# Reordering the first loads of a gated attention and token-MLP kernel: w1 tile 1 ahead of x tile 2, and the bias row off ScalarE's queue

## The chip, the cores and the metric

The kernel runs on one core of one Trainium2 chip. The metric is the device time of one execution in microseconds; before the change it is 163.06 us, the median of three runs that lie between 162.8 and 163.33. One further execution was recorded by the hardware profiler, and all times inside the kernel come from it. Its clock zero is the first instruction of the program.

## What is computed

An input x of 2048 rows and 512 columns (bf16) goes through two branches, and a gate per row mixes them.

```python
g = sigmoid((x * gate_w).sum(-1, keepdims=True))
a = linear_attention(x, wqkv, wo)          # 32 heads of 16
h = layernorm(x)                           # per row, over the 512 columns
u = gelu(einsum("bsd,sf->bdf", h, w1) + b1)   # w1: 2048 x 1792
y = einsum("bdf,fs->bds", u, w2) + b2
out = g * a + (1 - g) * transpose(y)
```

Only the start matters here: the layernorm of x, and the product of w1 with it, which contracts over the 2048 rows.

## The kernel before, in words

x, its layernorm and w1 are cut into 16 tiles of 128 rows. `xr[:, t, :]` is x tile t as loaded (128 KB), `xh[:, t, :]` the same tile after the layernorm. Of w1, the first 1024 columns are `w1A` (256 KB for each tile t), used by the first stage; the other 768 columns come later as `w1B`.

**TensorE** first does 18 matmuls on a constant (`warm_ps`). Then the first real stage fills eight accumulators `accA[j]`, j = 0 to 7, one for each 128 columns of w1A. For tiles t = 0 to 11 the loops run over t outside and j inside, so that eight matmuls in a row belong to one tile; the last four tiles are done per accumulator. A matmul (t, j) needs `w1A[:, t, 128 j : 128 j + 128]` as weights and `xh[:, t, :]` as data. All matmuls of the kernel are recorded by one helper and have line L74. The K projection, `kacc`, follows this stage.

**Loads.** All loads are recorded by one helper, line L124, and an engine issues its loads in program order. Nearly all are on SyncE's queue (SP). Ahead of the change SP issues x tile 0, x tile 1, the columns 128 to 1023 of w1A tile 0 (224 KB), then for t = 1 to 15 in turn x tile t+1 and w1A tile t (of tile 1 again only the columns 128 to 1023). b2's row follows w1A tile 4. Then come the gate's weights, the K weights and sixteen transposing loads of x (`xT`). ScalarE's queue (ACT) issues three loads at the start: b1's row, and the first 128 columns of w1A tiles 0 and 1 (32 KB each). Behind them ScalarE runs a square root on a constant (L137), which loads its table.

Each load signals on one of eight semaphores that are handed out in rotation over both queues, in the order of the loads in the built program; a ninth load is issued only after the one that had its semaphore before has landed.

**Layernorm, on VectorE and ScalarE, in an order written out by hand.** For a tile: statistics (`bn_stats`, L197), their sum (`bn_aggr`, L200), the standard deviation on ScalarE (L202), a reciprocal (L208) and the scaling that writes xh (L210). The statistics of the next tile are put between: for t = 1, 2, 3 they are cut in two halves of 256 columns, of which the first stands ahead of the scaling of the tile before.

```python
for t in range(1, NT):
    if t < HALVES:                      # HALVES = 4
        ln_bn(t, 0, D // 2, 0, 2)       # waits for x tile t
        ln_apply(t - 1)                 # reciprocal and scaling: writes xh of tile t-1
        ln_bn(t, D // 2, D, 1, 2)
    else:
        ln_bn(t, 0, D, 0, 1)
        ln_apply(t - 1)
    ln_aggr(t)
```

So on VectorE the first half of the statistics of x tile 2 stands ahead of the scaling of tile 1, and that of x tile 3 ahead of the scaling of tile 2. Behind the sum of tile 8 VectorE turns the two bias rows into columns (L232 to L234); they are first used by the GELU behind accumulator 0.

Of the kernel before, what the change touches and what calls it, by code (L numbers as in the profile page):

```python
# [15 lines left out]
def kernel(  # L16
# [13 lines left out]
    nc = tc.nc  # L30
    P = nc.NUM_PARTITIONS
# [9 lines left out]
    NT = S // P  # L41
    ND = D // P
    NF = F // P
# [4 lines left out]
    FA = NFA * P  # L48
# [5 lines left out]
    w1_view = B_w1.rearrange("(t p) f -> p t f", p=P)  # L54
    w2_view = B_w2.rearrange("(f p) s -> p f s", p=P)
    b1_view = B_b1.rearrange("(f p) -> f p", p=P)
# [9 lines left out]
    def ptile(shape, dt, name):  # L66
        return persist.tile(shape, dt, name=name, tag=name)
# [27 lines left out]
    b_rows = ptile([32, P], BF16, "b_rows")  # L95
# [22 lines left out]
    w1A = wpool.tile([P, NT, FA], BF16, name="w1A", tag="w1st")  # L118
# [4 lines left out]
    def load(o, i, eng=None, **kw):  # L123
        pin((eng or nc.sync).dma_start(out=o, in_=i, **kw))  # L124

    def load_x(t0, t1):
        load(xr[:, t0:t1, :], x_view[:, t0:t1, :])

    def load_w1a(t):
        load(w1A[:, t, :], w1_view[:, t, 0:FA])  # L130


    tbl = work.tile([P, 1], FP32, name="tbl", tag="tbl", bufs=2)
    load(b_rows[0:NF, :], b1_view, nc.scalar)
    load(w1A[:, 0, 0:P], w1_view[:, 0, 0:P], nc.scalar)
    load(w1A[:, 1, 0:P], w1_view[:, 1, 0:P], nc.scalar)
    pin(nc.scalar.activation(out=tbl[:], in_=eps_t[:], func=ACT.Sqrt))  # L137
# [1 line left out]
    load_x(0, 1)  # L139
    load_x(1, 2)  # L140
    load(w1A[:, 0, P:FA], w1_view[:, 0, P:FA])
    for t in range(1, NT):
        if t + 1 < NT:
            load_x(t + 1, t + 2)
        if t == 1:
            load(w1A[:, 1, P:FA], w1_view[:, 1, P:FA])
        else:
            load_w1a(t)
        if t == 4:
            load(b_rows[NF : NF + NT, :], b2_view)  # L150
    load(gw_b[:], gw_row_view.to_broadcast([P, D]))
    load(wk_sb[:], wqkv_view[:, :, D : 2 * D])
# [404 lines left out]
    t = NT - 1  # L557
# [35 lines left out]
```

## Time and profile before

| what | us |
|---|---|
| device time, median of 3 runs | 163.06 |
| span of the profiled execution, first to last instruction | 161.6 |
| difference of the two, for what lies outside the span | 1.5 |
| TensorE busy in the span | 157.1 |
| VectorE busy in the span | 118.7 |
| ScalarE busy in the span | 53.0 |

The profiler gives the span of its own execution; that execution's device time is not given separately, and 1.5 us is the difference of a median and a span. TensorE is busy 97% of the span at a granted clock of 0.998, so the time is the matmuls plus the few places where TensorE stands still. In the views, PE is TensorE, PEld its weight loads, DVE VectorE, ACT ScalarE, POOL GpSimd; SPq and ACTq are queues that issue loads.

### The profile page before, as it was taken

The numbers are of one execution on the slowest core, as the hardware profiler recorded it, in microseconds if no ns is written. First come the engines' busy times: TensorE is split into PE (matmuls) and PEld (weight loads), VectorE is DVE, ScalarE is ACT, GpSimd is POOL, SyncE is SP. The second block draws the span as 40 slices with busy tenths as digits, with TensorE's granted clock in tenths as the row PEclk, the third lists the DMA queues.
The fourth block names the chain that finished last, engine by engine and source line by source line (L and its number), as shares of the span: only waits on it lengthen the run. The fifth ranks groups of instructions, "written<-read, shape, count | busy, mean of one in ns | idle before, by whom it ended". The sixth has DMA issues, their size and how long they took to land.

```text
span 161.6 us, 2275 instructions
## 1 busy us (share of the span) xinstructions
PE 157.1 (97%) x820; PEld 72.9 (45%) x820; DVE 118.7 (73%) x279; ACT 53.0 (33%) x89; POOL 1.2 (1%) x8
## 2 busy tenths in 40 slices
PE   7899999999999999999999999999999999999993
PEld 5344444444444444444444444444444444444452
DVE  2799998959998998799895999999999980000002
ACT  3122226895243221435225970000008300550050
POOL 2000000000000000000000000000000000000000
PEclk9999999999999999999999999999999999999999
DMA  4999998444699540229953007826535925824421
GB/s 140 271 320 353 364 300 144 101 103 106 159 394 390 149 129 0 87 50 310 402 200 67 0 32 230 322 65 143 186 89 136 353 70 143 265 63 105 143 97 32
DMA packets 36966, 28.33 MB, mean 175 GB/s; under 512 B 20572, under 2 KB 31452, under 8 KB 36956
## 3 DMA queue, kind: packets, MB, share of 16 engines
q1 hardware_dynamic: 36368, 27.87, 57.0%
q10 hardware_dynamic: 588, 0.33, 0.7%
q8 instruction: 6, 0.10, 0.3%
q14 instruction: 4, 0.03, 0.1%
HBM read 19.28 MB, written 4.46 MB: 147 GB/s over the span
## 4 chain that ended last, share of the span: by engine, by line
PE 94%; DMA 3%; SPq 1%; DVE 0%; issue 0%; DVEq 0%
PE yps L74 39%; PE accA L74 16%; PE accB L74 13%; PE qacc L74 9%; PE Gps L74 9%; PE kacc L74 9%; DMA w1A<-in_B_w_dram 3%; SPq L124 1%; PE kvps L74 0%; DVE ot L537 0%; PE w2ps L74 0%; DVEq L537 0%
## 5 line engine op out<-in xcount | busy, mean ns | idle before, releaser
L74 PE MATMUL yps<-uT,w2h 128*128 128x512 bf16 (+2 forms) x238 | 49.2, 366 | 0.0
L74 PEld LDWEIGHTS <-w2h 128*128 128x128 bf16 x238 | 22.8, 98 | 25.9
L74 PE MATMUL accA<-xh,w1A 128*128 128x512 bf16 x128 | 28.0, 379 | 0.8 <-DVE xh L210 0.5
L530 ACT ACTIVATE ot<-yps,c,c 128x512 bf16<-128x512 f32 x15 | 11.6, 777 | 46.9 <-PE yps L74 35.5
L74 PE MATMUL accB<-xh,w1B 128*128 128x512 bf16 x96 | 21.5, 379 | 0.0
L537 DVE TENSOR_SCALAR ot<-yps,c,c 128x384 bf16<-128x384 f32 (+1 forms) x2 | 1.1, 545 | 25.5 <-PE yps L74 25.5
L74 PEld LDWEIGHTS <-w1A 128*128 128x128 bf16 x128 | 12.5, 98 | 16.1 <-DMA w1A<-in_B_w_dram 1.4
L74 PEld LDWEIGHTS <-xT 128*128 128x128 bf16 x128 | 12.4, 98 | 14.9 <-issue 0.2
L74 PE MATMUL kacc<-wk_sb,xT 128*128 128x512 bf16 x64 | 15.8, 379 | 0.0
L74 PE MATMUL Gps<-pk,xr 128*128 128x512 bf16 x64 | 15.8, 379 | 0.0
L74 PE MATMUL yps<-W2sb,pqT 128*128 128x512 bf16 (+2 forms) x68 | 14.6, 366 | 0.0
L74 PEld LDWEIGHTS <-w1B 128*128 128x128 bf16 x96 | 9.4, 98 | 11.3
L74 PE MATMUL qacc<-wq_sb,xT 128*128 128x512 bf16 x64 | 14.5, 379 | 0.0
L286 ACT ACTIVATE e<-qacc 128x512 bf16<-128x512 f32 x16 | 9.6, 597 | 12.2 <-DVE kvbdT L434 4.6
L286 ACT ACTIVATE e<-kacc 128x512 bf16<-128x512 f32 x16 | 9.2, 598 | 12.7 <-DVE pk L293 6.8
L197 DVE BATCH_NORM_STATS2 stats<-xr 128x6 f32<-128x512 bf16 (+1 forms) x19 | 11.1, 586 | 2.7 <-DMA xr<-in_A_x_dram 2.7
L288 DVE TENSOR_SCALAR e<-e 128x512 bf16<-128x512 bf16 x32 | 9.2, 288 | 4.6 <-ACT e L286 4.3
L406 DVE SCALAR_TENSOR_TENSOR pq<-pq,odds,rd 128x512 bf16<-128x512 bf16 x16 | 12.0, 752 | 0.6
L402 DVE TENSOR_REDUCE den<-prod 128x32 f32<-128x544 f32 x16 | 11.5, 720 | 0.6
L293 DVE SCALAR_TENSOR_TENSOR pk<-kacc,e 128x512 bf16<-128x512 f32 x16 | 11.1, 692 | 1.0
L293 DVE SCALAR_TENSOR_TENSOR pq<-qacc,e 128x512 bf16<-128x512 f32 x16 | 11.1, 692 | 0.6
L245 DVE CUSTOM_DVE_ANT_0 junk<-xr,gw_b 128x512 bf16<-128x512 bf16 x16 | 11.0, 689 | 0.4
(52 smaller groups left out, 95.0 us busy)
## 6 DMA issues: line engine op xcount, KB each, us to landing
w2h<-in_B_w_dram SPq DMA_DIRECT2D x3, 1792.0 KB, 7.5
w1A<-in_B_w_dram SPq DMA_DIRECT2D x14, 256.0 KB, 4.7
w1B<-in_B_w_dram SPq DMA_DIRECT2D x4, 768.0 KB, 6.2
xr<-in_A_x_dram SPq DMA_DIRECT2D x16, 128.0 KB, 4.1
q_dram<-pq SPq DMA_DIRECT2D x16, 128.0 KB, 3.7
out_dram<-ot SPq DMA_DIRECT2D x15, 128.0 KB, 1.8
w2h<-in_B_w_dram SPq DMA_DIRECT2D x1, 1280.0 KB, 6.5
wk_sb<-in_A_wqkv_dram SPq DMA_DIRECT2D x1, 512.0 KB, 6.5
```

The costliest lines, as they stand in the source:

```text
L74: nc.tensor.matmul(o, lhsT=lhsT, rhs=rhs, start=start, stop=stop, **kw)
L124: pin((eng or nc.sync).dma_start(out=o, in_=i, **kw))
L197: pin(nc.vector.bn_stats(out=stats[t][:, h, :], in_=xr[:, t, d0:d1]))
L245: nc.vector.tensor_tensor_reduce(out=junk[:], in0=xr[:, t, :], in1=gw_b[:], scale=1.0, scalar=0.0, op0=ALU.mult, op1=ALU.add, accum_out=gp ...
L286: pin(nc.scalar.activation(out=e[:], in_=acc[:], func=ACT.Exp))
L288: nc.vector.tensor_scalar(out=e[:], in0=e[:], scalar1=1.0, scalar2=PHI_EPS, op0=ALU.min, op1=ALU.add)
L293: nc.vector.scalar_tensor_tensor(out=o, in0=acc[:], scalar=0.0, in1=e[:], op0=ALU.max, op1=ALU.add)
L402: pin(nc.vector.tensor_reduce(out=den[:], in_=prod[:], op=ALU.add, axis=AX.X))
L406: nc.vector.scalar_tensor_tensor(out=heads, in0=heads, scalar=odds[:, t : t + 1], in1=rd[:].unsqueeze(2).to_broadcast([P, NH, HEAD]), op0= ...
L530: nc.scalar.activation(out=ot[:, d0:d1], in_=yps[:, d0:d1], func=ACT.Identity, scale=c1[:, t : t + 1], bias=c2[:, t : t + 1],)
L537: nc.vector.tensor_scalar(out=ot[:, d0:d1], in0=yps[:, d0:d1], scalar1=c1[:, t : t + 1], scalar2=c2[:, t : t + 1], op0=ALU.mult, op1=ALU.add,)
```

## The change

Three things are changed. On SP's queue the rest of w1A tile 1 (224 KB) is issued directly behind the rest of w1A tile 0, ahead of x tile 2, so that x tile 2 comes one place later; x tile 3 and all behind it keep their order. b1's row is no longer the first load of ScalarE's queue, which now begins with the first 128 columns of w1A tiles 0 and 1. b1's row is issued on SP instead, between w1A tile 4 and b2's row. The order of the instructions of TensorE and VectorE, and of the compute of ScalarE, stays as it was. The lines behind the edit move up by one.

```diff
     tbl = work.tile([P, 1], FP32, name="tbl", tag="tbl", bufs=2)
-    load(b_rows[0:NF, :], b1_view, nc.scalar)
     load(w1A[:, 0, 0:P], w1_view[:, 0, 0:P], nc.scalar)
     load(w1A[:, 1, 0:P], w1_view[:, 1, 0:P], nc.scalar)
     pin(nc.scalar.activation(out=tbl[:], in_=eps_t[:], func=ACT.Sqrt))
@@
     load_x(0, 1)
     load_x(1, 2)
     load(w1A[:, 0, P:FA], w1_view[:, 0, P:FA])
-    for t in range(1, NT):
+    load(w1A[:, 1, P:FA], w1_view[:, 1, P:FA])
+    load_x(2, 3)
+    for t in range(2, NT):
         if t + 1 < NT:
             load_x(t + 1, t + 2)
-        if t == 1:
-            load(w1A[:, 1, P:FA], w1_view[:, 1, P:FA])
-        else:
-            load_w1a(t)
+        load_w1a(t)
         if t == 4:
+            load(b_rows[0:NF, :], b1_view)
             load(b_rows[NF : NF + NT, :], b2_view)
```

## The prediction, on record before the changed kernel ran

> **What bounds the kernel now.** I read the chain of waits first. It says which piece of work ended last at each moment, from the start on.
>
> ```profile
> 51 pieces in order of time: start us, us, what
> ...
> 2.20 0.43 SPq L124
> 2.63 0.04 issue
> 2.67 4.65 DMA w1A<-in_B_w_dram
> 7.32 0.04 issue
> 7.37 25.86 PE accA L74 x119
> 33.23 4.32 PE kacc L74 x20
> ...
> 96.56 62.22 PE yps L74 x306
> 158.78 0.03 DVEq L537
> ```
>
> From 7.37 us to 158.78 us TensorE works without a hole; every link is PE. So whatever moves the point from which TensorE runs through moves the end by as much. What sets that point is a load of w1A that SP issues at 2.67 us and that lands at 2.67 + 4.65 = 7.32 us: the fifth load of SP's queue, the rest of w1A tile 1 ("w1r" below; "w0r" is that of tile 0). One matmul takes 25.86 / 119 = 0.217 us, the eight of a tile 1.74 us.
>
> Then the timeline of the first microseconds, for what stands just ahead of 7.37 (start, duration, engine; in brackets the idle time before it and who ended it).
>
> ```profile
> 2.92 0.69 DVE L197 BATCH_NORM_STATS2 stats<-xr 128x6 f32<-128x512 bf16 x1 [1.93 <-DMA xr<-in_A_x_dram]
> ...
> 4.49 0.41 DVE L210 TENSOR_SCALAR xh<-xr,mv,rstd 128x512 bf16<-128x512 bf16 x1
> ...
> 4.95 2.10 PE L74 MATMUL accA<-xh,w1A 128*128 128x512 bf16 x9 [0.50 <-DVE xh L210]
> ...
> 5.44 0.43 DVE L197 BATCH_NORM_STATS2 stats<-xr 128x6 f32<-128x256 bf16 x1
> ...
> 6.04 0.41 DVE L210 TENSOR_SCALAR xh<-xr,mv,rstd 128x512 bf16<-128x512 bf16 x1
> ...
> 7.37 18.95 PE L74 MATMUL accA<-xh,w1A 128*128 128x512 bf16 x87 [0.31 <-DMA w1A<-in_B_w_dram]
> 7.75 0.41 SPq L124 DMA_DIRECT2D w1A<-in_B_w_dram  x1
> 7.75 0.43 DVE L197 BATCH_NORM_STATS2 stats<-xr 128x6 f32<-128x256 bf16 x1 [0.72 <-DMA xr<-in_A_x_dram]
> ```
>
> TensorE does nine matmuls from 4.95 (eight of tile 0 and the first of tile 1, whose weights came by ScalarE's queue). The tenth would have started at 4.95 + 9 x 0.217 = 6.90 and starts at 7.37, so w1r costs 0.47 us; the view shows 0.31 because it counts the ninth's drain as busy. VectorE starts the statistics of x tile 2 at 5.44 and then scales tile 1, done at 6.45. It is idle for x tile 3 until 7.75.
>
> Last, how long single loads took, from the DMA view over 2.15 to 2.5 us, which holds the issues of w0r and x tile 2 (last column: us from issue to landing).
>
> ```profile
> w1A<-in_B_w_dram SPq DMA_DIRECT2D x1, 224.0 KB, 3.3
> xr<-in_A_x_dram SPq DMA_DIRECT2D x1, 128.0 KB, 3.2
> ```
>
> SP issues w0r at 1.72, x tile 2 at 2.20, w1r at 2.67 and x tile 3 at 3.15. They land at 5.0, 5.4, 7.3 and 7.75 (x3 took 4.6, by the same view over its issue): in the order of the queue, each behind the one before, by 0.4 (x2), 1.9 (w1r) and 0.4 us (x3). Issue is 0.47 us apart and landing 1.9, so the queue is backlogged there; what is put ahead of a load delays its landing by the transfer, not by the 0.47 us of issue.
>
> **The change, part by part.**
>
> (1) *w1r moves ahead of x2.* It now follows w0r, and x2 follows it. With a the step that w1r takes behind w0r, w1r lands at 5.0 + a and x2 at 5.0 + a + 0.4. Bounds of a: below, 224 KB at the best rate near by (391 GB/s in the slice from 8 to 9 us in the table by stretches) is 0.59 us; above, the 1.9 us that w1r took. w0r is the other load of this size and kind: x1 landed at 1.26 + 2.1 = 3.35, so w0r took 1.65 behind it, some 0.1 of it the 32 KB piece from ScalarE's queue. The two near rows are 1.55 and 1.9, the far one 0.59. I take 1.5, a little under the near pair, since part of the 1.9 looks like a slow spell that need not return in full.
>
> The Trainium skill (DMA: Bandwidth & Descriptors, section Latency and other measured facts) gives HBM access as 0.2 us on average and 2 us at high load. By the first a would be near 0.6 and the sum below near nothing; by the second the spell returns. The trace has 1.9 us at the place, which is nearer the second.
>
> (2) *The first half of x2's statistics stands ahead of tile 1's scaling on VectorE.* This wait is hidden now: x2 landed at 5.4, just as VectorE came to it. Afterwards VectorE arrives at about 5.3 and stands until x2 is there, and behind the waiting instruction are tile 1's reciprocal and scaling, which TensorE needs for all eight matmuls of tile 1. From x2's landing to the end of that scaling: 0.03 to start, then 5.44 to 6.45 = 1.01; the matmul starts 0.05 after it (4.90 to 4.95). So tile 1 starts at T1 = x2 + 1.09 and runs through, w1r having landed long before. Now, tile 1 effectively starts at 7.37 - 0.217 = 7.15. The change of the end is T1 - 7.15, that is x2 - 6.06. With a = 0.59, x2 = 6.0 and the change is -0.1; with a = 1.9, x2 = 7.3 and it is +1.2; with 1.5, x2 = 6.9 and it is +0.84.
>
> (3) *b1 leaves ScalarE's queue.* It was issued at 1.02 for 0.63 us and its place is worth 0.66. The two 32 KB pieces are issued 0.66 earlier, and so is the table load at 2.58. The first standard deviation (3.98, its input ready at 3.83, usual hand-over 0.03) can start 0.12 earlier, and so can the first matmul, at 4.83 in place of 4.95. The end gets none of this in the forecast, since tile 1 waits for x2; it counts only where x2 is early. The small pieces also get out of the way of w0r: 32 KB at the rate above is 0.08 us, b1 nothing much, so w0r and all behind it land up to 0.1 us sooner. Against it, the first piece now runs beside x0 and x1 and can hold them up by as much; only tile 0 would see that, which has 1 us to spare in the forecast. I take -0.1, bounds -0.15 and +0.1.
>
> (4) *b1 on SP behind w1 tile 4.* One more issue of about 0.4 us ahead of x6 and everything behind. With the eight semaphores in rotation, b1 now waits for w1r's landing, b2 for x2's and x6 for x3's (about 7.6), so x6 goes out at 7.8 or so in place of 7.34. It landed at 10.7 and is read at 11.53, a reading that itself moves later with VectorE; w1 tile 5 landed at 11.6 for a use at 14.1. The bias rows are read at 15.06, b2 landed at 6.18 + 4.3 = 10.5, and b1 in front of it not later than 11.5. Cost: nothing, hidden by TensorE's 1.74 us a tile against VectorE's 1.18. Were that cover gone, it would cost the 0.4 us once.
>
> (5) *What is late next.* After tile 1, VectorE needs about 1.65 us for the next scaling (8.69 to 10.34, a row with the same steps) against TensorE's 1.74, so tiles 2 and 3 follow with under 0.1 us in hand and I count no second stall; from tile 4 VectorE gains 0.5 us a tile. Bounds 0 and +0.2.
>
> Sum: 0.84 - 0.1 = +0.74 us on the span of 161.6, giving 162.3; the same 1.5 us lies around it, so the median goes from 163.06 to **163.8**.
>
> **The rivals.**
>
> *No spell.* w1r goes through at the steady rate, x2 lands at 6.0 and the change is -0.1 to +0.4 (a up to 1.1). For it: x4 (issued 4.10, 4.6 to landing) and x5 (5.16, 4.5) land 1.0 us apart, with the 256 KB of w1A tile 3 between them, so there a w1A load and an x load took 1.0 together. Against: both w1A loads of this stage took over 1.5 each. Time 163.0 to 163.4, taken as 163.1.
>
> *Faster.* The backlog is an accident of one recording: x2 lands by 5.5, as loads on an empty queue do (x0 and x1 took 2.1 us; x2, issued at 2.67, would be there at 4.8). Then VectorE never waits, tile 1 begins at 4.83 + 1.74 = 6.57 and runs on, and the second hole goes: -0.47 - 0.12 = -0.6 us, 162.5. It decides from x2 before 5.57, which needs w1r to pass in under 0.2 us. The four landings in queue order speak against it.
>
> *The clock drops.* TensorE would stand for about 1.3 us after tile 0. The 18 matmuls of 256 columns at the start took 3.62 us, 0.20 each, where later ones of 512 take 0.217: half rate. Were such a start repeated after the hole, it would lose half of 3.6 us: 163.8 + 1.8 = 165.6. The 0.49 us hole at 4.46 passed at a granted clock of 1.00, and no longer one is in this trace to tell. The Trainium skill (TensorE: Matmul & The Clock Gate, section Part 1: The HAM clock gate) puts the idle time that cools the array at about 3.4 us, so by that rule 1.3 us does nothing; no row here shows it.
>
> *The change not doing what it says.* Both queues carry the loads in the order of the diff in the built program and VectorE's order is the old one, so I give this nothing.
>
> **How the numbers follow.** What the runs can tell from no change is 0.3%, 0.49 us. Chances: forecast (a above 1.1, change +0.35 to +1.3) 0.57; no spell 0.31; faster 0.09; clock 0.03. In the forecast's case the change exceeds 0.49 with 0.88 of its chance, 0.50; with the clock's 0.03, slower has 0.53. Faster by over 0.49 is the faster case at 0.09. The rest, 0.38, is the same. The range takes in the forecast's case up to a = 1.9 with 0.1 of (3), 164.4, and the no-spell case down to 162.8; it leaves out the faster and the clock case and a little at the edges. The forecast's own range is 163.4 to 164.4.
>
> **What would show it.** (1) is right if w1r lands near 6.4 and x2 near 6.8, in that order; wrong if x2 lands before 6.1. (2) is right if VectorE's longest wait behind the first is for x tile 2, about 1.5 us, and TensorE's hole stands after eight matmuls and not nine, its releaser the scaling of tile 1 and not w1A; wrong if the hole is still released by w1A. (3) is right if the first matmul starts near 4.85. (4) is right if no wait in the stretch from 15 to 20 us names the bias rows. (5) is right if TensorE has no hole behind tile 1's. The prediction fails if x2 is not held up by w1r, or if the profiled execution before is no typical one: the hole at 7.37 rests on one slow load, and a median run may have had less of it.

## The result, and the profile after

The changed kernel takes 163.57 us, the median of 22 runs, against 162.99 us for 22 runs of the kernel before. One run of the changed kernel, at 165.69 us, is 1.3% above its median and is left out of the ratio. The ratio of the two is 1.0024 with a 95% interval of 1.0015 to 1.0034, which is 0.39 us (0.24 to 0.55): slower, by less than the 0.3% that the prediction had set as its bound. The forecast was 163.8 us, a ratio of 1.0045.

The chain of waits of the changed kernel, from the start, over 0 to 10 us (start, duration, what):

```profile
...
2.67 3.85 DMA xr<-in_A_x_dram
6.52 0.02 issue
6.54 0.43 DVE stats L196
6.97 0.07 DVE rstd L207
...
7.07 0.42 DVE xh L209
7.49 0.04 issue
7.53 2.53 PE accA L74 x11
```

Before, one link stood here, the load of w1A tile 1. Now the link is the load of x tile 2, landing at 6.52, and behind it come VectorE's statistics of that tile and then the scaling of tile 1. Only at 7.53 does TensorE begin tile 1. From there it runs through to the end as before.

The timeline of the same execution shows who waits:

```profile
3.15 0.69 DVE L196 BATCH_NORM_STATS2 stats<-xr 128x6 f32<-128x512 bf16 x1 [2.16 <-DMA xr<-in_A_x_dram]
...
5.09 2.28 PE L74 MATMUL accA<-xh,w1A 128*128 128x512 bf16 x8 [0.25 <-DVE xh L209]
...
5.68 1.41 PEld L74 LDWEIGHTS <-w1A 128*128 128x128 bf16 x8 [1.10 <-DMA w1A<-in_B_w_dram]
...
6.54 0.43 DVE L196 BATCH_NORM_STATS2 stats<-xr 128x6 f32<-128x256 bf16 x1 [0.93 <-DMA xr<-in_A_x_dram]
...
7.07 0.41 DVE L209 TENSOR_SCALAR xh<-xr,mv,rstd 128x512 bf16<-128x512 bf16 x1
```

VectorE stands 0.93 us for x tile 2. Two things are new beside it. x tile 0 is later (statistics at 3.15, not 2.92), and so is the first matmul (5.09, not 4.95). And the weights of the second matmul, the rest of w1A tile 0 (w0r), come only at 5.68: the eight matmuls of tile 0 take 2.28 us, where eight in a row take 7 x 0.217 + 0.38 = 1.9.

The place of the holes can be added up. The K projection's first matmul comes after all the accA work. With no hole behind the first matmul it started at 32.58 us (the second recording of before, below); in the first recording of before it started at 33.06, in the changed kernel at 33.43. Before lost 0.48, all by w1A tile 1. The changed kernel lost 0.85: 0.14 by the later first matmul, 0.37 between the first and the second matmul (5.68 - 5.09 - 0.217) and 0.33 at tile 1. The second matmul waits for w0r, but some 0.16 of the 0.37 would have been there in any case: TensorE was still at half rate, as shown below under "x tile 2 later still". All three losses lie ahead of 7.53, and x tile 2 alone sets 7.53.

### The profile page after: what moved, and what is told of

Read it like the earlier page. It is cut to its first block, busy times and chain, and to the rows that moved or that the text cites. A ratio compares the mean times of both kernels' runs of the same rounds, so it can differ in the third digit from the quotient of the medians.

```text
span 161.9 us, 2262 instructions
## 1 busy us (share of the span) xinstructions
PE 157.1 (97%) x806; PEld 73.1 (45%) x820; DVE 118.7 (73%) x279; ACT 53.1 (33%) x89; POOL 1.2 (1%) x8
## 4 chain that ended last, share of the span: by engine, by line
PE 93%; DMA 2%; SPq 1%; DVE 1%; issue 1%; DVEq 0%
PE yps L74 38%; PE accA L74 16%; PE accB L74 13%; PE kacc L74 9%; PE qacc L74 9%; PE Gps L74 8%; DMA xr<-in_A_x_dram 2%; SPq L124 1%; PE kvps L74 0%; DVE stats L196 0%; DVE xh L209 0%; DVE ot L536 0%; PE w2ps L74 0%; DVE rstd L207 0%; DVEq L536 0%
```

## The experiments

The theories at the start. **A**: x tile 2 behind w1r holds tile 1's scaling on VectorE, and that is the whole loss. **B**: the two 32 KB pieces on ScalarE's queue, issued sooner, hold up x tiles 0 and 1 and w0r, and that is the loss. **C**: both count.

**The SP order alone.**

The edit to before:

```diff
-    for t in range(1, NT):
+    load(w1A[:, 1, P:FA], w1_view[:, 1, P:FA])
+    load_x(2, 3)
+    for t in range(2, NT):
         if t + 1 < NT:
             load_x(t + 1, t + 2)
-        if t == 1:
-            load(w1A[:, 1, P:FA], w1_view[:, 1, P:FA])
-        else:
-            load_w1a(t)
+        load_w1a(t)
```

> Part (1) alone: SP's order as in the changed kernel, b1's row still first on ScalarE's queue. Theory A (x tile 2 behind w1r holds the scaling of tile 1 on VectorE, and that is the whole loss): slower than before by the same 0.3 to 0.5 us as the changed kernel, TensorE's hole behind eight matmuls and released by the scaling of tile 1, VectorE waiting 0.5 us or more for x tile 2. Theory B (the two 32 KB pieces, issued 0.7 us sooner, hold up x tiles 0 and 1 and w0r, and that is the loss): within 0.15 us of before. Theory C (both count about half): slower by about 0.2 us.

Ratio to before 1.0017 (1.0000 to 1.0033), medians 163.47 and 163.13. In its timeline the first statistics start at 2.88 and

```profile
4.96 2.10 PE L74 MATMUL accA<-xh,w1A 128*128 128x512 bf16 x8
...
6.56 0.43 DVE L196 BATCH_NORM_STATS2 stats<-xr 128x6 f32<-128x256 bf16 x1 [1.08 <-DMA xr<-in_A_x_dram]
...
7.55 1.89 PE L74 MATMUL accA<-xh,w1A 128*128 128x512 bf16 x8 [0.50 <-DVE xh L209]
```

Tile 0 is as early as in before, and tile 1 is as late as in the changed kernel, released by the scaling. A as expected. (This execution's span of 162.4 also holds 0.47 us of waiting for a w2 load at 130 us, which has nothing to do with the start.)

**b1's move alone.**

The edit to before:

```diff
-    load(b_rows[0:NF, :], b1_view, nc.scalar)
@@
         if t == 4:
+            load(b_rows[0:NF, :], b1_view)
```

> Parts (3) and (4) alone: b1's row on SP behind w1 tile 4, SP's order of x tile 2 and w1r as before. Theory A: within 0.1 us of before or up to 0.1 faster, x tile 0 landed within 0.05 us of 2.90 or the first matmul no later than 4.95. Theory B: slower by 0.3 to 0.5 us, x tile 0 landing near 3.13 as in the changed kernel and w0r near 5.6, with a hole behind the first matmul. Theory C: x tile 0 later by 0.2 us, slower by about 0.2 us.

Ratio 1.0010 (0.9997 to 1.0023): not told apart from no change, nor from 0.2 us. In the recording the first statistics start at 3.12, the first matmul at 5.05 and w0r lands at 5.45:

```profile
3.12 0.69 DVE L197 BATCH_NORM_STATS2 stats<-xr 128x6 f32<-128x512 bf16 x1 [2.12 <-DMA xr<-in_A_x_dram]
...
5.49 0.13 PEld L74 LDWEIGHTS <-w1A 128*128 128x128 bf16 x2 [0.92 <-DMA w1A<-in_B_w_dram]
...
5.90 0.15 PEld L74 LDWEIGHTS <-w1A 128*128 128x128 bf16 x1 [0.28 <-issue]
```

So the delay of x tile 0 and of w0r belongs to this part, as B and C had expected and A had not. The K projection starts at 33.18 here, 0.60 behind 32.58: 0.10 by the first matmul and 0.49 by the next three, which start at 5.50, 5.90 and 6.20. Of these only the second waits for w0r; the others are TensorE's half rate (below).

**The changed kernel with tile 1's scaling ahead of x tile 2's statistics.**

The edit to the changed kernel:

```diff
+            if t == 2:
+                ln_apply(t - 1)
             ln_bn(t, 0, D // 2, 0, 2)
-            ln_apply(t - 1)
+            if t != 2:
+                ln_apply(t - 1)
```

> The changed kernel with the reciprocal and scaling of tile 1 put ahead of the statistics of x tile 2 on VectorE, so that they no longer stand behind a wait for x tile 2. Theory A: the hole behind tile 0 goes or is left to w0r or w1r; faster than the changed kernel by 0.3 to 0.5 us and level with before or 0.1 faster. Theory B: within 0.1 us of the changed kernel, because tile 0's matmuls end only at 7.3 us for want of w0r. Theory C: faster than the changed kernel by about 0.2 us.

Ratio to before 1.0005 (0.9991 to 1.0019), median 163.17, against 163.57 and 163.40 for the changed kernel. Its timeline:

```profile
5.05 5.12 PE L74 MATMUL accA<-xh,w1A 128*128 128x512 bf16 x23 [0.22 <-DVE xh L209]
6.14 0.41 DVE L209 TENSOR_SCALAR xh<-xr,mv,rstd 128x512 bf16<-128x512 bf16 x1
6.47 0.75 DVE L196 BATCH_NORM_STATS2 stats<-xr 128x6 f32<-128x256 bf16 x2
```

The hole behind tile 0 is gone, though SP's order is that of the changed kernel. About 0.3 us of the loss hangs on the order on VectorE (1.0024 less 1.0005; the two intervals overlap a little). The medians carry this, more than the recording: x tile 2 landed at 5.92 in it, so that by the old order tile 1 would have started at about 5.92 + 1.01 = 6.93, only 0.15 later than the 6.78 that it did.

**The same order on VectorE in the kernel before.** The edit is the same, made to before.

> The kernel before with the same order on VectorE (scaling of tile 1 ahead of the statistics of x tile 2). All theories: the hole of before is released by w1r and not by the scaling, so no gain; level with before, or slower by up to 0.3 us where the scaling of tile 2 comes later than TensorE reaches tile 2, since the order leaves VectorE idle for about 0.4 us waiting for ScalarE's standard deviation. It tells whether the new order by itself costs or brings something in e3.

Ratio 1.0001 (0.9989 to 1.0014). The new order by itself brings and costs nothing that shows. In this recording w1r landed at 6.67, ahead of its use at 6.9: there was no hole at tile 1 at all.

**The kernel before, recorded again**, because that last row did not fit the first recording.

> The kernel before, unchanged, recorded once more. Theory S (the 1.9 us that w1r took in the first recording is an unlucky one of a spread, so that the recording had a hole of 0.47 us that a median run has not): w1r lands behind x tile 2 by 0.6 to 1.4 us, the hole released by w1A is under 0.2 us or gone, the span 161.1 to 161.4. Rival (the 1.9 us belongs to the place): w1r lands near 7.3 again, with the hole of 0.3 in the view and a span near 161.6. The ratio to before, 1.000, tells what the comparison can resolve.

Ratio to itself 1.0002 (0.9987 to 1.0018), which is what the comparisons here resolve. Its timeline and the DMA view over w1r's issue:

```profile
4.95 5.34 PE L74 MATMUL accA<-xh,w1A 128*128 128x512 bf16 x24
```

```profile
w1A<-in_B_w_dram SPq DMA_DIRECT2D x1, 224.0 KB, 4.1
```

w1r landed at 2.67 + 4.1 = 6.7 and TensorE has no hole behind its first matmul. Behind x tile 2, w1r took 1.69 us here and 1.26 in the run above, against 1.90 in the first recording. The first recording lay at the long end of the spread: its span of 161.6 and the 1.7 to 1.8 us that lie around a span in the runs where both are listed make some 163.3, 0.35 above the median.

Such spread is made ahead of the K projection. This execution took 162.81 us with the K projection at 32.58; in nine of the other recordings the time is 162.81 plus what the K projection starts later than 32.58, within 0.03 us. (With no small pieces it is 0.12 more, and the SP order alone has its wait for w2 besides.)

**The SP order with neither suspect**: the SP swap alone, with the scaling of tile 1 first, b1 still first on ScalarE's queue.

> SP's order of the changed kernel, b1's row first on ScalarE's queue as before, and the scaling of tile 1 ahead of the statistics of x tile 2 on VectorE: neither of the two suspected costs. If they are all there is: no hole behind the first matmul but at most 0.2 us at tile 2, level with before or faster by 0.1 to 0.3 us, and faster than the changed kernel by about 0.5. If SP's order costs in another way than by the wait on VectorE: slower than before by 0.2 us or more.

Ratio 1.0010 (0.9998 to 1.0022), median 163.20. The recording has no hole behind the first matmul, as expected (span 161.1):

```profile
4.96 4.48 PE L74 MATMUL accA<-xh,w1A 128*128 128x512 bf16 x20 [0.54 <-DVE xh L209]
```

Here, too, x tile 2 was early, at 5.96. The gain of 0.5 us over the changed kernel was not there, 0.2 to 0.4 by the medians; the interval leaves open whether some of SP's order costs on.

**x tile 2 later still.**

The edit to the kernel with the SP order alone (w1A tile 2 is not loaded again in the loop):

```diff
     load(w1A[:, 1, P:FA], w1_view[:, 1, P:FA])
+    load_w1a(2)
     load_x(2, 3)
```

> SP's order alone, with w1A tile 2 (256 KB) put ahead of x tile 2 as well, so that the suspected wait is about doubled. Theory A, in slope: x tile 2 lands 0.6 to 1.0 us later than with the swap alone, TensorE's hole behind tile 0 grows by as much, and the time is 0.6 to 1.0 us over the swap alone, 0.9 to 1.4 over before. Rival (the time does not hang on x tile 2's landing): under 0.3 us over the swap alone.

Ratio 1.0099 (1.0073 to 1.0125), 1.6 us over before and 1.1 over the swap alone by the medians: more than expected, in four runs. In the timeline:

```profile
7.35 0.43 DVE L198 BATCH_NORM_STATS2 stats<-xr 128x6 f32<-128x256 bf16 x1 [1.88 <-DMA xr<-in_A_x_dram]
...
8.35 1.02 PE L74 MATMUL accA<-xh,w1A 128*128 128x512 bf16 x4 [1.04 <-DVE xh L211]
```

x tile 2 landed 0.79 later than with the swap alone (7.33 against 6.54), tile 1 began 0.80 later (8.35 against 7.55) and the K projection 0.79 (34.24 against 33.45). One to one: this is the plainest support for A.

The same recording shows a loss of another kind at tile 0, though w0r had landed at 4.47:

```profile
5.33 0.15 PEld L74 LDWEIGHTS <-w1A 128*128 128x128 bf16 x1 [0.28 <-issue]
...
5.76 0.15 PEld L74 LDWEIGHTS <-w1A 128*128 128x128 bf16 x1 [0.28 <-issue]
6.06 0.96 PEld L74 LDWEIGHTS <-w1A 128*128 128x128 bf16 x5 [0.15 <-issue]
```

The second, third and fourth matmul start at 5.33, 5.76 and 6.06, and 0.43 is twice 0.217: TensorE is still at half rate. The warm-up's 18 matmuls of 256 columns take 4.00 us here, 0.213 apart to the last; in the first recording of before they take 3.62, and the last two start 0.11 apart. The trace's clock record, which the views do not print, has the full clock begin at 5.92 here, and between 3.84 and 6.06 over the 13 recordings. Where it begins behind the first real matmul, that costs tile 0 time: 0.46 us here, and 0.15 to 0.49 in five more. The views give a granted clock of 1.00 in these stretches too. In the changed kernel (full clock at 5.65) the wait for x tile 2 covers it. What sets the moment is not shown.

**The small pieces behind the table load.**

The edit to the kernel with b1's move alone:

```diff
-    load(w1A[:, 0, 0:P], w1_view[:, 0, 0:P], nc.scalar)
-    load(w1A[:, 1, 0:P], w1_view[:, 1, 0:P], nc.scalar)
     pin(nc.scalar.activation(out=tbl[:], in_=eps_t[:], func=ACT.Sqrt))
+    load(w1A[:, 0, 0:P], w1_view[:, 0, 0:P], nc.scalar)
+    load(w1A[:, 1, 0:P], w1_view[:, 1, 0:P], nc.scalar)
```

> b1's row on SP behind w1 tile 4 as in the changed kernel, SP's order of x tile 2 and w1r as before, and on ScalarE's queue the table load first and then the two 32 KB pieces, which so go out at about 2.3 and 2.7 us in place of 0.80 and 1.24. Theory B (it is the early pieces that hold up x tile 0): x tile 0 lands at 2.85 to 2.97 and the first scaling ends by 4.8, w0r lands earlier than in the run with b1 moved alone; level with that run or faster by 0.1 to 0.3 us unless the first piece itself comes late (then the first matmul waits for w1A near 4.9 to 5.1). Rival (x tile 0's 0.2 us have nothing to do with the pieces): x tile 0 lands at 3.1 again.

The edit did not do what was meant: the pieces went out at 1.05 and 1.48, not at 2.3, as the queue does not wait for the table load. The first statistics started at 3.05 and w0r landed at 5.63; ratio 1.0015 (1.0003 to 1.0027). It counts as one more place of the pieces, not as a test.

**The changed kernel, recorded again.**

> The changed kernel, unchanged, recorded once more. Theory C (two causes: x tile 2's wait on VectorE, and the earlier small pieces that delay x tile 0 and w0r): first matmul at 5.05 to 5.10, not 4.95; x tile 2 landing between 5.9 and 6.6, which puts the scaling of tile 1 between 6.9 and 7.6; w0r between 4.9 and 5.7; the ratio to before between 1.001 and 1.0035. If x tile 0 lands under 3.0 here, the delay of tile 0 in four recordings was chance.

Ratio 1.0021 (1.0006 to 1.0036). First statistics at 3.05, first matmul at 4.99 (a little ahead of the 5.05 to 5.10 expected), w0r at 5.51, x tile 2 at 6.46, tile 1 at 7.48:

```profile
4.99 0.38 PE L74 MATMUL accA<-xh,w1A 128*128 128x512 bf16 x1 [0.21 <-DVE xh L209]
...
5.56 1.68 PE L74 MATMUL accA<-xh,w1A 128*128 128x512 bf16 x7 [0.20 <-DMA w1A<-in_B_w_dram]
6.49 0.43 DVE L196 BATCH_NORM_STATS2 stats<-xr 128x6 f32<-128x256 bf16 x1 [0.98 <-DMA xr<-in_A_x_dram]
...
7.48 2.75 PE L74 MATMUL accA<-xh,w1A 128*128 128x512 bf16 x12 [0.23 <-DVE xh L209]
```

**No small pieces.**

The edit to the kernel with b1's move alone:

```diff
-    load(w1A[:, 0, 0:P], w1_view[:, 0, 0:P], nc.scalar)
-    load(w1A[:, 1, 0:P], w1_view[:, 1, 0:P], nc.scalar)
@@
-    load(w1A[:, 0, P:FA], w1_view[:, 0, P:FA])
+    load_w1a(0)
@@
-        if t == 1:
-            load(w1A[:, 1, P:FA], w1_view[:, 1, P:FA])
-        else:
-            load_w1a(t)
+        load_w1a(t)
```

> SP's order of before, no load on ScalarE's queue at all: b1's row on SP behind w1 tile 4, w1A tiles 0 and 1 whole (256 KB) on SP. The table load is as early as in the changed kernel and no small piece runs beside x tiles 0 and 1. Theory B (the pieces delay x tile 0): x tile 0 lands at 2.8 to 3.0 and its scaling ends at 4.75 to 4.85, 0.1 us before that of before; then the first matmul waits for the whole w1A tile 0, at 4.4 to 5.2 us. Rival (the removal of b1, or the earlier table load, delays x tile 0): x tile 0 lands at 3.1. Time: level with before, 0.1 faster to 0.3 slower.

Ratio 1.0014 (0.9999 to 1.0029). The timeline:

```profile
2.90 0.69 DVE L192 BATCH_NORM_STATS2 stats<-xr 128x6 f32<-128x512 bf16 x1 [1.91 <-DMA xr<-in_A_x_dram]
...
4.83 5.43 PE L74 MATMUL accA<-xh,w1A 128*128 128x512 bf16 x23
```

x tile 0 is back, with b1 away and the table load early. So neither of these delays it; the pieces do, as B says of x tile 0. And 4.83 is the start that the prediction had worked out for an early table load. In the recording the gain of 0.12 is lost again to the half rate: the second and third matmul start at 5.21 and 5.57, 0.16 and 0.31 us late, with w1A tile 0 landed at 4.52. Why the median of 163.29 is no better is not settled by one recording.

**x tile 2 first.**

The edit to the kernel with the SP order alone:

```diff
     load_x(1, 2)
+    load_x(2, 3)
     load(w1A[:, 0, P:FA], w1_view[:, 0, P:FA])
     load(w1A[:, 1, P:FA], w1_view[:, 1, P:FA])
-    load_x(2, 3)
```

> x tile 2 ahead of both w0r and w1r on SP (x0, x1, x2, w0r, w1r, x3), b1's row first on ScalarE's queue. Theory A: VectorE never waits for x tile 2, no hole behind tile 0 released by the scaling. Theory T (w1r takes over 1.2 us when it follows an x tile and 0.6 to 1.0 when it follows w0r): w1r lands 0.6 to 1.0 behind w0r. w0r itself lands up to 0.4 later than in before, near 5.2, so a hole of 0 to 0.5 us behind the first matmul. Time: level with before to 0.3 us slower. Rival to T (w1r is slow at its time of 4.4 to 5.5 whatever it follows): w1r lands 1.3 us or more behind w0r.

Ratio 0.9995 (0.9978 to 1.0012). w1r still stands directly behind w0r, as in the change, but x tile 2 no longer stands behind it, and no loss shows. w1r landed 0.60 behind w0r (5.86 against 5.26), as the theory about its step had it. (That theory, a long step behind an x tile, does not hold in general: with b1's move alone w1r landed at 6.35, about 0.55 behind x tile 2, by VectorE's start on that at 5.82.) The recording has a loss of 0.40 at 5.3 to 5.8:

```profile
5.30 0.18 PEld L74 LDWEIGHTS <-w1A 128*128 128x128 bf16 x2 [0.73 <-DMA w1A<-in_B_w_dram]
...
5.76 3.36 PEld L74 LDWEIGHTS <-w1A 128*128 128x128 bf16 x16 [0.28 <-issue]
```

The matmuls start at 4.95, 5.33 and 5.76, as at half rate with the weights there; w0r, 0.3 late, adds nothing that shows. No kernel here is faster than before beyond its interval.

## Why the prediction was right or wrong, point by point

The mechanism was right; the size was not. +0.74 us was forecast, +0.39 by the ratio (+0.58 by the medians) was measured. The time lies in the range.

**What bounds the kernel: the reading was right, the number not typical.** The hole of 0.47 us at w1r was real in that execution, but none of the five other recordings with the old SP order has a hole at w1A tile 1: where its landing is on record, it came at 6.35, 6.52 (the whole tile in one load), 6.67 and 6.74. What the change removes is worth 0.47 us in the first recording and nothing in those five. A median run of before still takes 0.2 us more than the fastest (162.99 against 162.8), but what those five recordings lose is lost at tile 0: by the half rate in three (0.15, 0.31 and 0.49) and by w0r in one (0.46). In the changed kernel the wait for x tile 2 covers such losses, so that it does not pay for them a second time. The prediction named the untypical recording as a way to fail, and did not put it into the sum.

**Step (1), the step a of w1r: this failed.** It was taken as 1.5 us, from the two loads near it. In four recordings with w1r directly behind w0r it was 0.80 (the SP order alone), 0.65, 0.97 and 0.60: the far row, 0.59, was nearer. Behind x tile 2 it was 1.90, 1.69 and 1.26, and about 0.55 with b1's move alone. So the slow spell did not move along with w1r. In the changed kernel w1r's own landing is not in the records; w1r and x tile 2 together took 0.88 and 0.95 us behind w0r, against 1.9 in the sum. A second miss hid this one: w0r was taken to land at 4.9 and landed at 5.64 and 5.51. So x tile 2 was forecast at 6.8 and came at 6.52 and 6.46, close by two errors of opposite sign (-1.0 and +0.7). In the three other recordings with this SP order it came at 6.54, 5.92 and 5.96, two of them ahead of the 6.1 that the prediction had set as the sign of being wrong.

Counted from an execution without a hole, in which tile 1 starts at 4.95 + 1.74 = 6.69, the prediction had the changed kernel lose 1.2 us (7.15 + 0.74 = 7.89) and the kernel before 0.47. The changed kernel lost 0.85 and 0.80 in its recordings: about 0.3 less by x tile 2's landing and 0.1 less by step (2). The kernel before lost 0.2 in a median run, and in the recordings by other causes. Both ends of the sum were too high, so part of the error cancelled, and that the time lies in the range is in part luck. The 1.5 us taken for what lies outside the span was also too small, by 0.2 to 0.3, which does not touch the change.

The table by stretches shows the slow spell itself; the columns that matter are the last two, the busy share of the DMA engines and GB/s. First the kernel before, then the changed one:

```profile
4.50:5.50 1.00, 0.55 (x3) 0.39 (x4) 0.97 (x4) 0.00 (x0) 0.00 (x0) 1.00 0.68 129
```

```profile
3.50:4.50 1.00, 1.00 (x7) 0.69 (x6) 0.92 (x4) 0.29 (x1) 0.00 (x0) 1.00 0.69 158
```

Before, the dip lies at 4.5 to 5.5, ahead of w1r's landing at 7.32; after, it lies a microsecond earlier, ahead of w0r's at 5.64. That the dip makes the next load late is read from this order in time, and no run tests it. With the SP order alone the same two stretches, 4.5 to 5.5 and 3.5 to 4.5, moved 316 and 348 GB/s; there x tile 2 was the slow one, 1.31 us behind w1r. What sets where the dip falls is open.

**Step (2), VectorE's order: right in kind and nearly in number.** x2 + 1.09 was forecast for tile 1's start; 1.01 and 1.02 were measured. The hole stood behind eight matmuls and was released by the scaling, as forecast; VectorE's wait was 0.93 and 0.98 us, not 1.5. Removing the order removed the loss; making x tile 2 later moved the end one to one. Theory A is what the changed kernel loses by, as far as these intervals tell.

**Step (3), b1 off ScalarE's queue: wrong in sign, with no effect at the end that shows.** -0.1 was taken. x tile 0's statistics started at 3.15, 3.05, 3.12 and 3.12 in the four recordings with the pieces issued at 0.80, and at 2.82 to 3.03 in the seven with b1 ahead of them; 2.90 with no pieces. Theory B thus holds for x tile 0, and the bound of +0.1 was a little too low (+0.14 and +0.04 at the first matmul). The Trainium skill says it in DMA: Bandwidth & Descriptors, section Issuing engines are not separate DMA queues: loads of different issuing engines run on the same 16 DMA engines and interleave. The trace agrees: the means of those starts are 3.11 and 2.91, so two loads of 32 KB cost the 128 KB of x tile 0 some 0.2 us. w0r, too, was late in four of five recordings with early pieces (5.45 to 5.64, once 4.97) and landed at 4.43 to 5.01 in six with b1 first and w0r in its old place; why so late is not shown. In the changed kernel tile 0 itself is covered, because tile 1 waits for x tile 2 beyond it. But x tile 2 lands behind w0r in the queue, and whether it would have come sooner without the early pieces is open: the SP order alone, without them, had it as late (6.54) and loses as much (1.0017 against 1.0024 and 1.0021, intervals that overlap).

**Steps (4) and (5): right.** No wait in 15 to 20 us names the bias rows; behind tile 1 TensorE has no hole, with the scaling of tile 2 done at 9.03 for a use at 7.53 + 1.74 = 9.27. The load of x tile 6 went out at 7.08, earlier than the 7.8 worked out, as x tile 3 landed at 6.93.

**The rivals.** "No spell" priced a rightly, but reckoned from the long recording and with w0r on time, so its 163.1 was too low. "Faster" did not come: x tile 2 never landed before 5.9 behind w1r. The clock did not drop: the run with x tile 2 later still left TensorE idle for 1.04 us in the view, and the matmuls behind it are 0.21 to 0.22 apart, the full rate. (The granted clock of the views cannot show this, as it reads 1.00 at half rate too.) This fits the rule of the Trainium skill that the prediction cited (TensorE: Matmul & The Clock Gate, section Part 1: The HAM clock gate: an idle time of about 3.4 us cools the array) without testing it at its edge. What the prediction did not think of is that TensorE may not yet have reached the full rate at tile 0.

## What to carry to other kernels

When two loads of a backlogged queue change places, follow the one that becomes later into the program order of its reader: what stands behind the waiting instruction there is what it costs. And a hole that rests on one slow load is a draw from a spread: a kernel is judged by its median, so its holes should be read from a second recording, or from the same wait in other runs, before their removal is booked. A slow row is not a property of the load that it is written beside; in its new place the same load took 0.60 to 0.97 us. Last, a wait covers the delays ahead of it: here x tile 2's wait covered a late w0r and the half rate, so that what a single hole seems to cost is not what the kernel gains when it goes.

## What was not expected of the hardware

The same 224 KB load took 1.26 to 1.90 us behind an x tile in three recordings, about 0.55 in a fourth, and 0.60 to 0.97 directly behind another w1 load in four. Two loads of 32 KB on another queue, issued at 0.80 and 1.24 us, delayed the reader of a 128 KB load issued at 0.80 by 0.2 us in the mean (3.11 against 2.91). And TensorE went from half to full rate anywhere from 3.84 to 6.06 us, with the same warm-up matmuls in every recording; in six of the 13 this cost 0.15 to 0.49 us of the first tile.
